# Late blocks of a token and channel MLP: the seventh second-layer product as seven of half size, and the last row's x by way of device memory

## The chip, the cores and the metric

The kernel runs on one core of one Trainium2 chip. The metric is device time in microseconds; lower is better. TensorE is called PE in the profile (PEld: its weight loads), VectorE DVE, ScalarE ACT, GpSimd POOL, SyncE SP.

## The reference

Eight batch rows. For each, eight heads of attention over 576 tokens with 64 elements each: the scores are scaled, those that lie more than tau under the row's largest are dropped, the rest goes through a softmax, and the weights multiply v. The heads side by side are x, 576 tokens by 512. Then an MLP over tokens, one over channels, both with a residual:

```
scores = scale * q @ k.T
scores = where(scores >= max(scores) - tau, scores, -1e9)
attn   = softmax(scores) @ v
x      = attn, heads side by side            # (8, 576, 512)
u      = x + (relu(x.T @ w_tok1) @ w_tok2).T # tokens: 576 -> 256 -> 576
out    = u + relu(u @ w_ch1) @ w_ch2         # channels: 512 -> 1536 -> 512
```

All of it is in 32-bit floats.

## The kernel before

**Main part.** Attention and the token MLP run row by row, 1 core, with tokens along the free dimension (`xT`, 128 x 4 x 576, holds x and then u of a row). A scheduler written into the kernel (`Scheduler`) holds every operation with a cost, a rank and its dependences, keeps a modelled clock per engine, and picks what can start first; the order in which it picks is the order of instructions on each engine. Nothing is reordered at run time: an engine that waits holds all that is queued behind it.

**The channel MLP is put off.** `NOW` says how many groups of 256 tokens of a row take it at once: two for row 0, one for rows 1 to 6, none for row 7. What is left of u is written to device memory by `spill(b)` (L533), except for row 7, whose u stays in `xTs[7]`.

**Late blocks.** After attention, when its memory is free, what was put off runs in five blocks of 512 tokens each (class `Late`, L1440): tokens of rows 1 and 2, rows 3 and 4, the last 64 tokens of all eight rows, rows 5 and 6, and row 7's first 512. `load` (L1448) fetches a block's u into one buffer `u`; the block of row 7 is marked `own` and reads `xTs[7]` in place. `turn_u` and `move_u` lay u out by tokens into `us` and `ut` for the residual.

**First layer** (`make_first`, L1530). For each of six slices j, the 2 x 2 product of halves is made with seven products and a number of sums (Strassen's scheme in Winograd's form) instead of eight products. Four sums of u (`sum_u`, buffer `t`) and three of the weights (`w1s`) feed it. Results, after relu, lie in `ga` (first half of the hidden layer) and `hidden_b` (second half).

**Second layer** (`make_second`, L1582). Again seven products. With a(i, k, m) the hidden activations (token half i, hidden half k, m one of two tiles of 128 tokens), the sums are S1 = a(1,0) + a(1,1), S2 = S1 - a(0,0), S3 = a(0,0) - a(1,0) and S4 = a(0,1) - S2. S1 and S2 have places of their own (`sum_place(0, m)` and `sum_place(1, m)`, in the memory of `x_sb` and `a`), S3 lies in a(1,0)'s place and S4 in a(0,1)'s. Six of the seven products are themselves made by `make_inner` (L1703) as seven products of half width and half depth, 3 matrix multiplies of 128 x 128 x 128 each (four of the six in the last block, where the products with a(0,0) and S1 are of full size). `make_inner` has the same scheme inside: its sums s1 to s4 are taken in place, on quarters of the left operand, one after another as the products that read them are done; its small results p1, u2, u3 lie in `small_place`, of which there are two sets, and its three weight sums in `inner_place(n)`, made once on DVE before the first second layer; the weights' quarter (0,1) is overwritten in place. The product x2 = a(0,1) times `side2(1, 0)` is the one that is of full size in all blocks: 6 matrix multiplies of 128 x 128 x 256 for each m. It stands first in the second layer, DVE adds it and the residual into o(0,0) (`y2`), and S4 is then taken in place:

```
x2[m] = plain(lambda m=m: a(0, 1, m), lambda: side2(1, 0), h2)
y2[m] = put_leave("dve", 0.42, lambda bank, m=m: add(four(o(0, 0, m)), four(bank), old(0, 0, m)), x2[m], ...)
s4[m] = sched.op("dve", 0.96, lambda m=m: sub(a(0, 1, m), a(0, 1, m), sum_place(1, m)), s2[m] + [x2[m]], 3)
```

Products fill eight PSUM banks; ACT or DVE takes each result out, and a bank is free for the next product when that is done.

Of the kernel before, what the change touches and what calls it, by code (L numbers as in the profile page):

```python
# [21 lines left out]
def kernel(  # L22
# [1127 lines left out]
    def make_row(b):  # L1150

        deps = [key_op("X", rank_of_group(b, p0, g)) for p0 in (0, 2) for g in range(3)]
        halves = make_tokens(b, token_mlp(b) if b else token_mlp(0, range(NP // 2, NP)), deps)
        if not b:
            for k in ("20", "21"):
                halves[k] = first_half[k] + halves[k]
        t = [x for x in sched.ops if x.eng == "pe" and x.row == b]
        tokens_x["1"] = [x for k, x in keyed.items() if k[0] == "tok" and k[1] == b and len(k) == 3]
        tokens_x["2"] = list(tokens_x["1"])
        outs = halves["20"] + halves["21"]  # L1160
        xreads[b] = xreads.get(b, []) + make_groups(b, halves) + outs
        if b < B - 1:
            xreads[b].append(put(("spill", b), sched.op("sp", 0.6, lambda: spill(b), outs, 2, dmas=(1, 383, 0.58))))
# [186 lines left out]

    flat = x_sb.rearrange("p t x -> p (t x)")
# [7 lines left out]
    def small_place(n, k):  # L1359
        if n == 0:  # L1360
            return small_a[:, k, :]
        return flat[:, 3 * TILE + P * k : 3 * TILE + P * k + P] if k < 2 else home("a")[:, TILE : TILE + P]

    def inner_place(n):
        at = [
            lambda: inner[0].rearrange("p k j x -> p (k j x)"),
            lambda: w1.rearrange("p t x -> p (t x)")[:, 0:QUARTER],
            lambda: w2.rearrange("p t x -> p (t x)"),
            lambda: home("xT")[:, 0:QUARTER],
            lambda: inner[1].rearrange("p k j x -> p (k j x)"),  # L1370
            lambda: inner_b.rearrange("p k j x -> p (k j x)"),
        ][n]()
        return at.rearrange("p (k j x) -> p k j x", k=3, j=HH)
# [7 lines left out]
    FACTORS = [lambda: w2s[:, 2], lambda: w2s[:, 1], lambda: side2(0, 1), lambda: side2(1, 1), lambda: side2(0, 0), lambda: w2s[:, 0]]  # L1381
# [9 lines left out]
    tokens = [x for x in pending if x.row == B - 1]  # L1391
# [12 lines left out]
    for n, y in enumerate(FACTORS):  # L1404
        quarter = lambda q, r, y=y: y()[:, HH * q : HH * q + HH, P * r : P * r + P]
        s = lambda k, n=n: inner_place(n)[:, k]
        steps = [
            lambda s=s, y=quarter: sub(s(0), y(0, 1), y(0, 0)),
            lambda s=s, y=quarter: sub(s(1), y(1, 1), s(0)),
            lambda s=s, y=quarter: sub(s(2), y(1, 0), s(1)),  # L1410
            lambda s=s, y=quarter: sub(y(0, 1), y(1, 1), y(0, 1)),
        ]
        done = []
        for step in steps:
            done.append(sched.op("dve", 0.55, step, free_all + done, 9))
        inner_weights.append(done)
# [21 lines left out]
    small_used = [[], []]  # L1438

    class Late:  # L1440


        def __init__(self, n):
            self.n = n
            self.own = groups[n][0][0] == B - 1
            self.us, self.ut, self.products = [None, None], [None, None], {}

        def load(self):  # L1448
            self.u = end.tile([P, NCC, 2 * GR], F32, tag="u", bufs=1, name=f"u_{self.n}")
            at = 0  # L1450
            for b, lo, n in groups[self.n]:
                src = spilled[b][:, :, lo - GR * NOW[b] :][:, :, 0:n] if b in spilled else xTs[b][:, :, lo : lo + n]
                nc.sync.dma_start(out=self.u[:, :, at : at + n], in_=src)
                at += n
# [11 lines left out]
        def block(self, k, n):  # L1466
            u = xTs[B - 1] if self.own else self.u
            return u[:, HC * k : HC * k + HC, GR * n : GR * n + GR]
# [13 lines left out]
        def turn_u(self, m, n):  # L1482
            pool = work if m == 0 else end
            if n == 0:
                self.us[m] = pool.tile([P, 2, 4, NCC * 32], F32, tag="us", bufs=1, name=f"us_{self.n}_{m}")
                self.ut[m] = pool.tile([P, 2, 4, NCC * 32], F32, tag="ut", bufs=1, name=f"ut_{self.n}_{m}")
            u = xTs[B - 1] if self.own else self.u
            nc.vector.transpose(
                out=self.us[m][:, n].rearrange("q a (c d) -> q c a d", c=NCC),
                in_=u[:, :, GR * n + P * m : GR * n + P * m + P].rearrange("q c (r a) -> q c a r", a=4),  # L1490
            )
# [5 lines left out]
        def make(self, before, spills):  # L1497
# [3 lines left out]
            if self.own:  # L1501
                ready = list(tokens)
            else:
                slots = [x for x in before if not x.own]
                free = slots[-1].reads if slots else []
                came = [spills[b] if b < B - 1 else x for b, _, _ in groups[n] for x in (tokens if b == B - 1 else [None])]
                count = len(groups[n])
                ready = [sched.op("sp", 1.2, self.load, came + free, -1, dmas=(count, 1024 // count, 0.6))]
# [16 lines left out]
            for j in range(HJ):  # L1525
                self.make_first(hidden, j, ready + sums, past.freed if past else {(i, k): free_all for i in range(2) for k in range(2)})
# [3 lines left out]
        def make_first(self, hidden, j, have, free):  # L1530
# [33 lines left out]
            z = put_bank(C, product(lambda: ws(0), lambda: us(0)), held((1, 1), (1, 0)) + [c6], rank)  # L1564
            x7 = put_more(y, C, product(lambda: w(1, 0), lambda: us(2), False), [c6] + have, 2)
            c7 = put_mid("act", 0.37, copy_to(u3), y, [x7] + used, 0)
            d5 = put_mid("dve", 0.42, lambda bank: add(gb(1), bank[:, 0:GR], u3), z, [z, c7] + free[1, 1])
            x4 = put_more(y, C, product(lambda: w(1, 1), lambda: us(3), False), [c7] + held((0, 1)), 2)
# [13 lines left out]
        def make_second(self, hidden, moved):  # L1582
# [59 lines left out]
            for m in range(2):  # L1642
                x2[m] = plain(lambda m=m: a(0, 1, m), lambda: side2(1, 0), h2)
                y2[m] = put_leave("dve", 0.42, lambda bank, m=m: add(four(o(0, 0, m)), four(bank), old(0, 0, m)), x2[m], [x2[m]] + moved[m])
                s4[m] = sched.op("dve", 0.96, lambda m=m: sub(a(0, 1, m), a(0, 1, m), sum_place(1, m)), s2[m] + [x2[m]], 3)
            ends = self.n == len(groups) - 1
            if ends:
                whole = []
                for n in (4, 5):
                    back = lambda q, r, n=n: FACTORS[n]()[:, HH * q : HH * q + HH, P * r : P * r + P]  # L1650
                    whole.append(sched.op("dve", 0.55, lambda back=back: sub(back(0, 1), back(1, 1), back(0, 1)), past_sums, 4))
                for m in range(2):
                    x1.append(plain(lambda m=m: a(0, 0, m), lambda: side2(0, 0), h11 + whole[:1]))
                    c1[m] = [put_leave("act", 0.37, lambda bank, m=m: nc.scalar.copy(out=p1_place(m), in_=bank[:, 0:HD]), x1[m], [x1[m]] + past_sums, 0)]
            else:
                c1 = self.make_inner(4, lambda m: a(0, 0, m), p1_place, [h11, h11], s2[0] + s2[1] + s3[0] + s3[1], [past_sums, past_sums])
                w5 = self.make_inner(5, lambda m: sum_place(0, m), lambda m: o(1, 1, m), s1, s2[0] + s2[1], [moved[0], moved[1]])
            w7_of = lambda m: w7[:, m, :]
            w4 = self.make_inner(0, lambda m: a(1, 1, m), lambda m: o(1, 0, m), [h2, h2], s1[0] + s1[1], [moved[0], moved[1]])
            w6 = self.make_inner(1, lambda m: sum_place(1, m), w6_place, s2, s4, [past_sums, past_sums])  # L1660
            w7s = self.make_inner(2, lambda m: a(1, 0, m), w7_of, s3, [], [past_sums, past_sums])
            w3 = self.make_inner(3, lambda m: a(0, 1, m), lambda m: o(0, 1, m), [[s4[0]], [s4[1]]], x2, [moved[0], moved[1]])
            all_second = []
            for m in range(2):
# [10 lines left out]
                if ends:  # L1675
                    b11 = joined(lambda eng, m=m: add(old(1, 1, m), old(1, 1, m), four(w7_of(m)), eng), [u3] + moved[m])
                    x5 = plain(lambda m=m: sum_place(0, m), lambda: w2s[:, 0], whole[1:] + s1[m] + small_used[0] + small_used[1][:1])
# [20 lines left out]
                (0, 1): x2 + s4 + self.products[3],  # L1698
# [4 lines left out]
        def make_inner(self, n, x, to, have, freed, writable):  # L1703
# [18 lines left out]
            p1, u2, u3 = [lambda k=k: small_place(n % 2, k) for k in range(3)]  # L1722
            used = small_used[n % 2]
# [31 lines left out]
            small_used[n % 2] = [d6, d7, d5, d4, d3]  # L1755
# [4 lines left out]
    spills = [key_op("spill", b) for b in range(B - 1)]  # L1760
# [36 lines left out]
```

## Time and profile before

| | us |
|---|---|
| median of 3 runs | 1220.56 |
| lowest, highest | 1220.19, 1221.44 |
| profiled execution, whole | 1218.91 |
| its span, first to last instruction | 1217.1 |
| PE busy in the span | 1191.5 |
| PE weight loads | 971.7 |
| DVE busy | 885.7 |
| ACT busy | 601.6 |
| POOL busy | 334.9 |

The span is that of one profiled execution; what lies around it, 1.8 us, is the difference to that execution's own time. Matrix multiplies are pipelined: each has a length in the trace, but the next one begins before it ends, so that the distance between two starts is what one costs. A row of the timeline puts equal instructions together and gives their count; one matrix multiply of the code is two instructions there. Of a group's row the numbers are: busy time, mean length of one in ns, idle time of the engine just before, and what ended it. The first late block begins at 862.73 us.

### The profile page before, as it was taken

What the parts mean: (1) busy time and instruction counts of PE and PEld (TensorE: products, weight loads), DVE (VectorE), ACT (ScalarE), POOL (GpSimd) and SP (SyncE); (2) the same over time, 40 slices, a digit from 0 to 9 for tenths busy, and PEclk for the clock granted to TensorE, in tenths of its full rate; (3) what the DMA queues carried; (4) which work ended last, traced back from release to release, by engine and by line L of the source; (5) the groups of instructions that cost most, each with busy time, mean ns of one, the idle gap of its engine ahead of it and who ended that gap; (6) DMA issues with size and microseconds to landing.
All of it is one profiled execution on the core that took longest, in us unless ns stands there. A gap on an engine that the chain in (4) does not pass through costs nothing.

```text
span 1217.1 us, 21941 instructions
## 1 busy us (share of the span) xinstructions
PE 1191.5 (98%) x7913; PEld 971.7 (80%) x7913; DVE 885.7 (73%) x1497; ACT 601.6 (49%) x1360; POOL 334.9 (28%) x524
## 2 busy tenths in 40 slices
PE   8888999999999999999999999999999999999998
PEld 8656788777777777777777777778899898999988
DVE  7788996677778677767866876742677586776856
ACT  6988864564656565465556566431232323223130
POOL 3676543333333424433333333410100000000000
PEclk9999999999999999999999999999999999999999
DMA  8656867768777776776876875850210302120010
GB/s 147 138 124 171 230 170 164 159 138 189 162 171 152 184 159 156 191 165 138 196 166 131 189 177 118 198 139 22 53 36 1 91 15 70 35 54 17 31 40 36
DMA packets 325372, 149.78 MB, mean 123 GB/s; under 512 B 223824, under 2 KB 318032, under 8 KB 325264
## 3 DMA queue, kind: packets, MB, share of 16 engines
q1 hardware_dynamic: 323104, 147.64, 53.0%
q8 instruction: 63, 1.03, 0.3%
q10 hardware_dynamic: 2160, 0.74, 0.2%
q14 instruction: 45, 0.37, 0.1%
HBM read 47.32 MB, written 13.50 MB: 50 GB/s over the span
## 4 chain that ended last, share of the span: by engine, by line
PE 85%; DVE 6%; ACT 2%; SPq 2%; DMA 2%; issue 1%; POOL 1%; ACTq 0%; DVEq 0%; POOLq 0%
PE bank L1436 29%; PE bank L1060 12%; PE sc L850 11%; PE bank L984 11%; PE bank L371 9%; PE bank L478 5%; PE bank L460 5%; PE bank L366 3%; DVE mx L867 2%; SPq L328 1%; DVE T L316 1%; PE warm L677 1%; ACT e L883 1%; DMA eT<-T 1%; POOL e L286 1%
## 5 line engine op out<-in xcount | busy, mean ns | idle before, releaser
L286 POOL TENSOR_SCALAR e<-e,rr 128x576 f32<-128x576 f32 x288 | 219.0, 780 | 210.5 <-DVE rr L278 197.4
L883 ACT ACTIVATE e<-sc,bias 128x576 f32<-128x576 f32 x288 | 194.7, 743 | 161.9 <-POOL bias L873 160.8
L893 ACT ACTIVATE e<-e,ntau 128x576 f32<-128x576 f32 x288 | 220.7, 780 | 0.2
L867 DVE TENSOR_REDUCE mx<-sc 128x2 f32<-128x1152 f32 x144 | 187.9, 1345 | 40.7 <-PE sc L850 40.4
L316 DVE STREAM_TRANSPOSE T<-e 128x1152 f32<-128x1152 f32 x126 | 170.4, 1362 | 38.5 <-DMA eT<-T 17.3
L1060 PE MATMUL bank<-xT,wc 128*128 128x256 f32 x768 | 178.1, 383 | 2.7 <-ACT g L1065 1.6
L1060 PEld LDWEIGHTS bank<-xT,wc 128*128 128x128 f32 x768 | 142.7, 190 | 31.2 <-issue 4.4
L850 PE MATMUL sc<-kT,qT 64*128 64x192 f32 (+1 forms) x1920 | 165.0, 332 | 1.4 <-ACT e L883 1.0
L850 PEld LDWEIGHTS sc<-kT,qT 64*128 64x128 f32 (+1 forms) x1920 | 138.0, 176 | 30.9 <-issue 19.1
L371 PE MATMUL bank<-eT,lv 128*64 128x384 f32 (+1 forms) x1024 | 135.1, 406 | 0.0
L371 PEld LDWEIGHTS bank<-eT,lv 128*64 128x64 f32 x1024 | 73.6, 137 | 50.6 <-issue 45.6
L873 POOL TENSOR_SCALAR bias<-mx,toff 128x2 f32<-128x2 f32 x144 | 41.3, 287 | 168.7 <-DVE mx L867 165.0
L984 PE MATMUL bank<-wc,g 128*128 128x256 f32 x336 | 77.9, 382 | 0.0
L478 PE MATMUL bank<-w,a 128*128 128x192 f32 (+1 forms) x256 | 72.9, 418 | 3.1 <-DVE g L1068 1.3
L984 PEld LDWEIGHTS bank<-wc,g 128*128 128x128 f32 x336 | 62.9, 190 | 13.2 <-issue 2.5
L460 PE MATMUL bank<-x_sb,w 128*128 128x256 f32 x320 | 72.5, 381 | 1.0 <-DVE x_sb L445 0.7
L1557 ACT COPY temps<-bank 128x256 f32<-128x256 f32 x90 | 33.4, 371 | 78.2 <-PE bank L1436 78.1
L460 PEld LDWEIGHTS bank<-x_sb,w 128*128 128x128 f32 x320 | 60.2, 190 | 10.6 <-DVE x_sb L445 1.0
L478 PEld LDWEIGHTS bank<-w,a 128*128 128x128 f32 x256 | 43.4, 189 | 22.7 <-issue 3.9
L1065 ACT ACTIVATE g<-bank 128x256 f32<-128x256 f32 x56 | 21.6, 385 | 80.4 <-PE bank L1060 79.4
L893 ACT ACTIVATION_READ_ACCUMULATOR e<-e,ntau 128x1 f32 x288 | 58.8, 204 | 0.0
L984 PE MATMUL bank<-w2s,g 128*128 128x256 f32 x252 | 58.2, 381 | 0.0
(180 smaller groups left out, 1811.2 us busy)
## 6 DMA issues: line engine op xcount, KB each, us to landing
eT<-T SPq DMA_DIRECT2D x504, 144.0 KB, 3.0
w2s<-in_moe_w_ch_dram SPq DMA_DIRECT2D x24, 512.0 KB, 4.1
lk<-in_k_dram SPq DMA_DIRECT2D x122, 72.0 KB, 2.8
ut<-us SPq DMA_DIRECT2D x136, 64.0 KB, 2.1
lq<-in_q_dram SPq DMA_DIRECT2D x120, 72.0 KB, 3.0
lv<-in_v_dram SPq DMA_DIRECT2D x112, 72.0 KB, 2.5
out_dram<-us SPq DMA_DIRECT2D x30, 256.0 KB, 2.3
spill<-xT SPq DMA_DIRECT2D x6, 640.0 KB, 4.1
```

The source lines that it names most:

```text
L286: nc.gpsimd.tensor_scalar(out=eh, in0=eh, scalar1=rr[:, h : h + 1], scalar2=1.0, op0=ALU.mult, op1=ALU.mult)
L316: nc.vector.transpose(out=T.rearrange("p a (c x) -> p c a x", c=NK), in_=e.rearrange("p (c a x) -> p c a x", c=NK, a=4))
L371: nc.tensor.matmul(to[r], lhsT=lv[:, j, :], rhs=e[j], start=False, stop=(c == NI - 1), skip_group_check=True)
L460: nc.tensor.matmul(to, lhsT=w1[:, t, P * m : P * m + P], rhs=x(t), start=(t == 0), stop=(t == NT - 1), skip_group_check=len(products) > 1,)
L478: nc.tensor.matmul(bank[:, n * i : n * i + n], lhsT=hidden[b][:, m, P * c : P * c + P], rhs=w2[:, m, lo : lo + n], start=(m == 0), stop=(m ...
L850: nc.tensor.matmul(sc[h][rows, f, HT * k : HT * k + HT], lhsT=qT[r, cols], rhs=kT[r, HT * f : HT * f + HT], start=True, stop=True, skip_gr ...
L867: nc.vector.tensor_reduce(out=mx[:, h], in_=sc[h][:, :, 0 : 2 * HT].rearrange("p f (k x) -> p k f x", k=2), axis=AX.XY, op=ALU.max)
L883: nc.scalar.activation(out=eh, in_=part[h], func=AF.Prelu, bias=bias[:, h], scale=SCALE, alpha=STEEP)
L893: nc.scalar.activation(out=eh, in_=eh, func=AF.Exp, bias=ntau, accum_out=rs[:, h, 0:1])
L984: nc.tensor.matmul(bank[:, 0:HD], lhsT=x[:, j, :], rhs=y[:, j, :], start=j == 0, stop=j == HJ - 1)
L1060: nc.tensor.matmul(bank[:, 0:n], lhsT=wc1[:, j, c, :], rhs=uT[:, c, GR * i : GR * i + n], start=(c == 0), stop=(c == NCC - 1))
L1436: nc.tensor.matmul(to, lhsT=l, rhs=r, start=start and x == 0, stop=x == len(pairs) - 1, skip_group_check=not start)
```

## The change

In the four blocks before the last, the product a(0,1) times `side2(1, 0)` is made by `make_inner` too, as number 6: per block, 12 matrix multiplies of 256 columns become 21 of 128, with sums on DVE and copies on ACT as the other six have. The last block keeps it at full size, and there the overwritten quarter of `side2(1, 0)` is restored first, as for the two others (`whole`).

Because the new product needs a(0,1) unchanged by S4 while it is made, S4 now goes into S1's place, after all products of S1 (number 5) are done; in the last block it stays in a(0,1)'s place (`of3` in the diff is the place that holds S4).

The weight sums of the new product need memory. Row 7's u is written to device memory as the others' is (`spill` for all rows), the blocks with row 7 load it from there, `own` goes, and the second buffer of `xT` becomes `late_y`, which holds these weight sums and three more sets of small places (five in all; products 0 to 6 use sets 0, 1, 0, 1, 2, 3, 4).

Beside that, in the first layer each product waits for the one sum of u that it reads instead of for all four, and the second product of a slice comes after the first.

```diff
-        if b < B - 1:
-            xreads[b].append(put(("spill", b), sched.op("sp", 0.6, lambda: spill(b), outs, 2, dmas=(1, 383, 0.58))))
+        xreads[b].append(put(("spill", b), sched.op("sp", 0.6, lambda: spill(b), outs, 2, dmas=(1, 383, 0.58))))
...
+    def home_of_last():
+        if "y" not in homes:
+            homes["y"] = work.tile([P, NP, S], F32, tag="xT", name="late_y").rearrange("p c x -> p (c x)")
+        return homes["y"]
...
+        if n > 1:
+            return home_of_last()[:, QUARTER + P * (3 * n - 6 + k) : QUARTER + P * (3 * n - 6 + k) + P]
...
+            lambda: home_of_last()[:, 0:QUARTER],
...
-    FACTORS = [lambda: w2s[:, 2], ..., lambda: w2s[:, 0]]
+    FACTORS = [lambda: w2s[:, 2], ..., lambda: w2s[:, 0], lambda: side2(1, 0)]
...
-            done.append(sched.op("dve", 0.55, step, free_all + done, 9))
+            done.append(sched.op("dve", 0.55, step, free_all + done + ([key_op("spill", B - 1)] if n == 6 else []), 9))
...
-    small_used = [[], []]
+    SMALL = [0, 1, 0, 1, 2, 3, 4]
+    small_used = [[] for _ in range(5)]
...
-                src = spilled[b][:, :, lo - GR * NOW[b] :][:, :, 0:n] if b in spilled else xTs[b][:, :, lo : lo + n]
+                src = spilled[b][:, :, lo - GR * NOW[b] :][:, :, 0:n]
...
-            x2 = put_bank(C, product(lambda: w(0, 1), lambda: u(1, 0)), held((0, 0)), rank)
+            x2 = put_bank(C, product(lambda: w(0, 1), lambda: u(1, 0)), held((0, 0)) + [y], rank)
...
-            x6 = put_more(y, C, product(lambda: ws(1), lambda: us(1), False), [c1] + have, 2)
+            x6 = put_more(y, C, product(lambda: ws(1), lambda: us(1), False), [c1, sums[1]] + have, 2)
...
-            for m in range(2):
-                x2[m] = plain(lambda m=m: a(0, 1, m), lambda: side2(1, 0), h2)
-                y2[m] = put_leave("dve", 0.42, ...)
-                s4[m] = sched.op("dve", 0.96, lambda m=m: sub(a(0, 1, m), a(0, 1, m), sum_place(1, m)), s2[m] + [x2[m]], 3)
...
             if ends:
...
-                for n in (4, 5):
+                for n in (6, 4, 5):
...
+                for m in range(2):
+                    x2[m] = plain(lambda m=m: a(0, 1, m), lambda: side2(1, 0), h2 + whole[:1])
+                    y2[m] = put_leave("dve", 0.42, ...)
+                    s4[m] = sched.op("dve", 0.96, lambda m=m: sub(a(0, 1, m), a(0, 1, m), sum_place(1, m)), s2[m] + [x2[m]], 3)
...
             else:
-                c1 = self.make_inner(4, lambda m: a(0, 0, m), p1_place, ...)
                 w5 = self.make_inner(5, lambda m: sum_place(0, m), lambda m: o(1, 1, m), s1, ...)
+                for m in range(2):
+                    s4[m] = sched.op("dve", 0.96, lambda m=m: sub(sum_place(0, m), a(0, 1, m), sum_place(1, m)), s2[m] + h2 + self.products[5], 2)
+                c1 = self.make_inner(4, lambda m: a(0, 0, m), p1_place, ...)
+                w2 = self.make_inner(6, lambda m: a(0, 1, m), lambda m: o(0, 0, m), [h2, h2], s4, [moved[0], moved[1]])
+                for m in range(2):
+                    y2[m] = joined(lambda eng, m=m: add(four(o(0, 0, m)), four(o(0, 0, m)), old(0, 0, m), eng), w2[m] + moved[m])
...
-            w3 = self.make_inner(3, lambda m: a(0, 1, m), ..., x2, [moved[0], moved[1]])
+            w3 = self.make_inner(3, of3, ..., read3, [moved[0], moved[1]])
...
-    spills = [key_op("spill", b) for b in range(B - 1)]
+    spills = [key_op("spill", b) for b in range(B)]
```

More of the change, by code (lines that the diff above doesn't have):

```diff
@@ L1390 @@
     last = [x for x in pending if x.row < B - 1]
-    tokens = [x for x in pending if x.row == B - 1]
     free_all = pending + state["stores"] + state["adds"]
@@ L1466, in block @@
         def block(self, k, n):
-            u = xTs[B - 1] if self.own else self.u
-            return u[:, HC * k : HC * k + HC, GR * n : GR * n + GR]
+            return self.u[:, HC * k : HC * k + HC, GR * n : GR * n + GR]
         def sum_u(self, n):
@@ L1500, in make @@
             past = before[-1] if before else None
[L1501 to L1508, printed above, removed]
+            free = before[-1].reads if before else []
+            came = [spills[b] for b, _, _ in groups[n]]
+            count = len(groups[n])
+            ready = [sched.op("sp", 1.2, self.load, came + free, -1, dmas=(count, 1024 // count, 0.6))]
             self.reads = []
@@ L1525, in make, with make_first @@
             for j in range(HJ):
-                self.make_first(hidden, j, ready + sums, past.freed if past else {(i, k): free_all for i in range(2) for k in range(2)})
+                self.make_first(hidden, j, ready, sums, past.freed if past else {(i, k): free_all for i in range(2) for k in range(2)})
             self.reads += sums + self.first
             self.make_second(hidden, moved)
-        def make_first(self, hidden, j, have, free):
+        def make_first(self, hidden, j, have, sums, free):
             rank = 3 + 2 * self.n
@@ L1641, in make_second @@
             x1 = []
-            for m in range(2):
-                x2[m] = plain(lambda m=m: a(0, 1, m), lambda: side2(1, 0), h2)
-                y2[m] = put_leave("dve", 0.42, lambda bank, m=m: add(four(o(0, 0, m)), four(bank), old(0, 0, m)), x2[m], [x2[m]] + moved[m])
-                s4[m] = sched.op("dve", 0.96, lambda m=m: sub(a(0, 1, m), a(0, 1, m), sum_place(1, m)), s2[m] + [x2[m]], 3)
             ends = self.n == len(groups) - 1
+            w7_of = lambda m: w7[:, m, :]
+            rests = [past_sums, past_sums]
             if ends:
                 whole = []
-                for n in (4, 5):
+                for n in (6, 4, 5):
                     back = lambda q, r, n=n: FACTORS[n]()[:, HH * q : HH * q + HH, P * r : P * r + P]
@@ L1652, in make_second @@
                 for m in range(2):
-                    x1.append(plain(lambda m=m: a(0, 0, m), lambda: side2(0, 0), h11 + whole[:1]))
+                    x2[m] = plain(lambda m=m: a(0, 1, m), lambda: side2(1, 0), h2 + whole[:1])
+                    y2[m] = put_leave("dve", 0.42, lambda bank, m=m: add(four(o(0, 0, m)), four(bank), old(0, 0, m)), x2[m], [x2[m]] + moved[m])
+                    s4[m] = sched.op("dve", 0.96, lambda m=m: sub(a(0, 1, m), a(0, 1, m), sum_place(1, m)), s2[m] + [x2[m]], 3)
@@ L1697, in make_second @@
                 (1, 1): flat_of(s1) + self.products[0],
-                (0, 1): x2 + s4 + self.products[3],
+                (0, 1): s4 + (self.products[6] if 6 in self.products else x2 + self.products[3]),
             }
@@ L1721, in make_inner @@
             weights = inner_weights[n]
-            p1, u2, u3 = [lambda k=k: small_place(n % 2, k) for k in range(3)]
-            used = small_used[n % 2]
+            p1, u2, u3 = [lambda k=k: small_place(SMALL[n], k) for k in range(3)]
+            used = small_used[SMALL[n]]
             def product(l, r, start=True):
```

28 lines of the change are left out of this document (14 added, 14 removed).

## The prediction

> **What bounds the kernel now.** I read the page first: its totals, the slices, the engines' shares of the chain that ended last.
>
> ```profile
> span 1217.1 us, 21941 instructions
> PE 1191.5 (98%) x7913; PEld 971.7 (80%) x7913; DVE 885.7 (73%) x1497; ACT 601.6 (49%) x1360; POOL 334.9 (28%) x524
> ...
> PE   8888999999999999999999999999999999999998
> ...
> PE 85%; DVE 6%; ACT 2%; SPq 2%; DMA 2%; issue 1%; POOL 1%; ACTq 0%; DVEq 0%; POOLq 0%
> ```
>
> TensorE (PE) carries 85% of the chain. The built order of the changed kernel equals that of before on every engine up to the first late block, so only the late stage matters. There, busy time by stretch (columns: stretch, its length, then busy time and instructions of PE, PEld, DVE, ACT, POOL, the clock, DMA share, GB/s); the last row is one whole middle block.
>
> ```profile
> 802.70:862.70 60.00, 60.00 (x284) 49.70 (x283) 19.71 (x28) 7.99 (x19) 4.51 (x5) 1.00 0.20 59
> 904.20:1038.50 134.30, 134.30 (x866) 124.62 (x865) 96.17 (x224) 38.48 (x107) 0.00 (x0) 1.00 0.15 40
> 1108.00:1190.00 82.00, 81.89 (x525) 75.88 (x524) 59.53 (x135) 22.33 (x62) 0.00 (x0) 1.00 0.10 27
> 1038.50:1108.10 69.60, 69.60 (x446) 64.57 (x445) 50.21 (x117) 19.68 (x55) 0.00 (x0) 1.00 0.19 46
> ```
>
> PE is never empty there, at full clock. DVE is busy 50.21 of 69.60 us and ACT 19.68. So the end moves by what PE has to do, plus what it must wait for. The timeline of PE gives the prices (start, length, then what; each matrix multiply of the code stands as two instructions):
>
> ```profile
> 862.73 1.89 PE L1436 MATMUL bank<-u,wc 128*128 128x256 f32 x8
> ...
> 1108.08 5.34 PE L1436 MATMUL bank<-wc,hidden_b 128*128 128x256 f32 x24
> 1113.26 1.03 PE L1436 MATMUL bank<-xT,wc 128*128 128x256 f32 x4
> 1114.12 0.83 PE L1436 MATMUL bank<-inner,ga 128*128 128x128 f32 x6
> 1114.79 0.83 PE L1436 MATMUL bank<-wc,ga 128*128 128x128 f32 x6
> ...
> 1210.04 2.75 PE L1436 MATMUL bank<-w2s,x_sb 128*128 128x256 f32 x12
> ```
>
> Lengths overlap; starts count. The product that is replaced (24 instructions, both halves m) holds PE from 1108.08 to 1113.26, 5.18 us, 0.216 per instruction. One half-size product (6 instructions of 128 columns) goes from 1114.12 to 1114.79, 0.67. A first-layer product of 4 instructions takes 0.86.
>
> **The sum on PE.** Each of the four blocks before the last gives up 5.18 us and gets seven times 0.67 = 4.69, so 0.49 less, four times: 1.96 us. The last block keeps the full-size form. No PE work is added elsewhere.
>
> How much idle time is there besides? A late block's first layer has 6 x 7 products at 0.86: 181 us for five blocks. Full-size products are 5 x 5.18 plus 2 x 5.18 in the last block, 36.3. Half-size ones: 4 x 42 + 28 = 196 at 0.67, 131.3. Together 348.6 us. The stage runs from 862.73 to 1210.04 + 2.59 = 1212.63: 349.9 us. So about 1.3 us is idle or rounding, and that is all that a better order could give on top.
>
> **What the seven add on DVE and ACT.** Per block: four sums over quarters, four small sums out of banks, one small sum, three copies on ACT. The sum of the old y2 stays (from SBUF instead of from a bank), and so does S4.
>
> ```profile
> L951 DVE TENSOR_TENSOR ga<-ga 128x384 f32<-128x384 f32 x10 | 5.4, 553 | 0.2
> L948 DVE TENSOR_TENSOR us<-us,ut 128x256 f32<-128x256 f32 x6 | 2.5, 422 | 0.2
> L948 DVE TENSOR_TENSOR small_a<-bank,small_a 128x128 f32<-128x128 f32 x6 | 1.7, 290 | 0.7 <-PE bank L1436 0.6
> L951 DVE TENSOR_TENSOR hidden_b<-hidden_b,x_sb 128x768 f32<-128x768 f32 x1 | 0.9, 950 | 0.0
> L948 DVE TENSOR_TENSOR late_x<-late_x,small_a 128x128 f32<-128x128 f32 x1 | 0.3, 281 | 0.0
> L1738 ACT COPY small_a<-bank 128x128 f32<-128x128 f32 x14 | 3.7, 266 | 6.7 <-PE bank L1436 6.6
> ```
>
> DVE: 4 x 0.553 + 4 x 0.290 + 0.281 = 3.65 us, so 53.9 of some 69.1 us. ACT: 3 x 0.266 = 0.8 us. Both lie beside PE work on average. The question is where DVE must answer in time, and the built order shows two tight places in each of the four blocks.
>
> First place: S4 now stands where S1 stood, so it may start only when all seven products of S1 are done, and the sums inside the new product come after it. In the built order 17 DVE operations lie between the sixth product of S1 and the fifth of the new one: ten small (2.9), four of 256 columns (1.7), the two S4 (1.9), the first quarter sum (0.55). Back to back that is 7.05 us. PE does in that time 5 half-size and 6 first-layer products, 5 x 0.67 + 6 x 0.86 = 8.5 us, of which the first 0.94 is gone before DVE can use the sixth product:
>
> ```profile
> 1049.68 0.83 PE L1436 MATMUL bank<-inner,ga 128*128 128x128 f32 x6
> ...
> 1050.62 0.62 DVE L948 TENSOR_TENSOR small_a<-bank,small_a 128x128 f32<-128x128 f32 x2 [0.33 <-PE bank L1436]
> ```
>
> So 7.05 us of DVE in 7.57: half a microsecond to spare, and I cost this at nothing. The cover is thin, though.
>
> Do operations on DVE take their whole length, one after the other?
>
> ```profile
> 1042.07 1.02 DVE L951 TENSOR_TENSOR ga<-ga 128x384 f32<-128x384 f32 x2
> 1074.40 0.56 DVE L948 TENSOR_TENSOR hidden_b<-hidden_b 128x384 f32<-128x384 f32 x1 [0.73 <-PE bank L1436]
> 1074.99 0.56 DVE L951 TENSOR_TENSOR hidden_b<-hidden_b 128x384 f32<-128x384 f32 x1
> 1075.81 0.62 DVE L948 TENSOR_TENSOR small_a<-bank,small_a 128x128 f32<-128x128 f32 x2 [0.26 <-PE bank L1436]
> 1076.46 0.29 DVE L948 TENSOR_TENSOR w<-bank,small_a 128x128 f32<-128x128 f32 x1
> ```
>
> Two that do not depend on each other begin 0.47 us apart (1.02 - 0.55), a dependent one 0.59 after the first. So 7.05 is about right or a little long.
>
> Second place: the sixth product inside the new one is followed after two others by its third, which waits for three small DVE sums. The same pattern exists today:
>
> ```profile
> 1074.87 0.83 PE L1436 MATMUL bank<-w,ga 128*128 128x128 f32 x6
> ...
> 1076.88 0.86 PE L1436 MATMUL bank<-wc,ga 128*128 128x128 f32 x6
> ```
>
> The sixth starts at 1074.87, its sums at 1075.81, the last sum ends at 1076.75, and the third product starts at 1076.88 instead of 1074.87 + 3 x 0.67 = 1076.88, its 0.86 showing 0.03 lost. Four more such places: 0.12 us. Where DVE is still at something else, it costs more:
>
> ```profile
> 1145.37 0.83 PE L1436 MATMUL bank<-wc,hidden_b 128*128 128x128 f32 x6
> 1146.31 0.94 PE L1436 MATMUL bank<-late_x,hidden_b 128*128 128x128 f32 x6
> ...
> 1146.30 0.74 PEld L1436 LDWEIGHTS bank<-late_x,hidden_b 128*128 128x128 f32 x6 [0.29 <-DVE small_a L948]
> ```
>
> Here PE lost 0.27 us (0.94 between starts against 0.67) behind a small sum. That was in the block whose second layer changes order, so it may go or come again; with its own length, 0.94 against 0.83, it lost 0.37. I take between 0 and 0.37 for each of the four blocks and 0.05 as the value, nearest to the 0.03 row: 0.2 us, ends 0 and 1.5.
>
> **What moves besides.** The last row's x goes out to device memory and comes back:
>
> ```profile
> 863.64 0.55 DVE L489 TENSOR_TENSOR xT<-xT,bank 128x384 f32<-128x384 f32 x1
> 867.60 10.27 SPq L1495 DMA_DIRECT2D ut<-us  x16
> 899.18 1.22 SPq L1453 DMA_DIRECT2D u<-spill  x2
> ...
> u<-spill SPq DMA_DIRECT2D x6, 512.0 KB, 4.6
> ```
>
> The spill can be issued at 864.2, behind the sum at 863.64. On SP it precedes the 16 moves, whose results are not read for 30 us. Its 1.18 MB should land within 4.6 x 1180/512 = 10.6 us, by 875. Who waits: on DVE the four quarter differences of the new product's weights, which overwrite that x; in the built order they stand near the end of block 0's first layer, after 890. Behind them on DVE are the last sums of that layer. Cost nothing; were the landing 10 us later still, PE would stop. The last block no longer reads x in place but loads it (two issues, 4.6 us), as blocks 1 and 3 do now behind the previous first layer, some 5 us ahead of its first sums: nothing. The four weight differences (2.2 us of DVE in block 0) and one restoring difference in the last block lie beside PE. The five sets of small places remove waits that the rows do not show as PE's idle time: nothing.
>
> At the start of each second layer PE had 5.18 us that needed no sum; now four half-size products, 2.68 us.
>
> ```profile
> 1038.47 5.34 PE L1436 MATMUL bank<-wc,hidden_b 128*128 128x256 f32 x24
> ...
> 1039.79 1.03 DVE L948 TENSOR_TENSOR x_sb<-ga,hidden_b 128x384 f32<-128x384 f32 x2 [0.70 <-ACT ga L1556]
> ```
>
> The first product that needs one of the last sums of S1 is three more on, 4.7 us in, and today these sums are done at 1040.82, 2.4 us into the layer. Nothing.
>
> Sum: -1.96 + 0.2 = -1.8 us (ends -2.0 and -0.5, or -3 with all idle gone). Against the profiled execution, span 1217.1, it is 1215.3; that execution took 1218.91 in all, 1.65 under the median of the runs, so I apply the difference to the median: 1220.56 - 1.8 = **1218.8**. That is 0.15%, inside the 0.2% (2.4 us) that a measurement of this kernel can tell from no change.
>
> **Rivals.** (a) The order improves as well: the idle 1.3 us, the two rows at 1146 among it, goes to below half. Then -1.96 - 0.7 or more, 1217.9 or lower: faster by over 0.2%. For it: the sums' waits are now given one by one, so that PE has more to choose from. Against: new tight places. Chance 0.16.
>
> (b) DVE sets the pace at the first tight place. If its 17 operations take 0.1 us more each (as dependent ones do beside independent ones, 0.59 against 0.47), 1.7 us, PE waits 1.2 us in each of four blocks: -1.96 + 4.8, 1223.4, slower. It decides from 1.1 us per block on. Against it: the half microsecond to spare, counted with full lengths. Chance 0.08.
>
> (c) Stalls of 0.3 to 0.5 us per block, as at 1146, eat the gain: 1220 to 1220.6, no change. Chance 0.10.
>
> (d) Halving the width does not halve the time, because each narrow product has as many weight loads. Were a half-size product paced by loads that do not overlap, the 0.74 us of the loads' row above instead of 0.67, seven would cost 5.18, the full-size price, and the change would gain nothing on PE and lose its stalls: 1220.8. The 0.67 between starts stands all through the stage, loads included, so 0.01. The Trainium skill, TensorE: Matmul & The Clock Gate, section Back-to-back issue gap, speaks for this rival: it gives measured 81 ns per product at 128 columns and 131 ns at 512, far from proportional. An estimate from it, by a straight line between, is 98 ns at 256 columns, so that seven half-size products would cost 1.45 times the full-size one. The trace does not agree: 0.112 us against 0.216 per instruction here.
>
> **The numbers.** The forecast itself has 0.65. Faster 0.16 (a); same 0.65 + 0.10 + 0.01 = 0.76; slower 0.08 (b). The range runs from the low side of (a), 1217.8, to the far end of (c), 1220.6; it leaves out (b) and some of (a).
>
> **What would show it.** In the changed trace: the two rows of 24 instructions on hidden_b gone from four blocks and in each a group `late_y,hidden_b`; middle blocks about 69.1 us instead of 69.6; PE busy throughout, last product ending near 1210.8. DVE some 54 us per block. I am wrong if PE shows idle time before the products on `late_y,hidden_b` or behind the S4 sums, if DVE waits for the spill before writing `late_y`, or if the middle blocks differ by other than half a microsecond.

## The result, and the profile after

The changed kernel takes 1216.96 us (median of 15 runs; before, 15 runs beside them, 1219.84): 0.9977 of before, 95% interval [0.9966, 0.9988]. Timed again later it was 0.9984 [0.9972, 0.9996]. So it is faster, by about 2 to 3 us, more than the 1.8 us of the forecast, whose range (from 1217.8) it leaves on the low side. The forecast counted from 1220.56, the median of three runs; the 15 runs of the kernel before lie 0.72 us lower. Against them the gain is 2.88 us.

The page of the profiled execution (1216.17 us in all) against the lines of before:

```profile
span 1214.4 us, 22144 instructions
PE 1189.0 (98%) x7985; PEld 971.5 (80%) x7985; DVE 901.6 (74%) x1538; ACT 603.4 (50%) x1372; POOL 333.8 (27%) x524
...
PE   8888999999999999999999999999999999999998
...
PE 84%; DVE 2%; ACT 1%; DMA 0%; SPq 0%; issue 0%; DVEq 0%; POOL 0%
```

PE has 72 more instructions (four times 42 in place of 24) and is 2.5 us less busy. DVE has 16 us more. The row by stretch (same columns as before) of the block that corresponds to the forecast's middle block:

```profile
1037.40:1106.50 69.10, 69.10 (x464) 64.62 (x463) 53.17 (x125) 20.20 (x57) 0.00 (x0) 1.00 0.19 47
```

69.10 us instead of 69.60, as forecast, and DVE 53.2 (forecast 53.9). The timeline of PE in the changed kernel (start, length, what): the start of the late stage, some of the half-size products that stand for the row of 24 instructions, and the last product:

```profile
862.80 1.89 PE L1442 MATMUL bank<-u,wc 128*128 128x256 f32 x8
...
1060.64 1.03 PE L1442 MATMUL bank<-t,w1s 128*128 128x256 f32 x4
1061.50 0.83 PE L1442 MATMUL bank<-late_y,hidden_b 128*128 128x128 f32 x6
...
1065.04 0.83 PE L1442 MATMUL bank<-late_y,hidden_b 128*128 128x128 f32 x6
...
1067.05 0.83 PE L1442 MATMUL bank<-wc,hidden_b 128*128 128x128 f32 x6
...
1207.59 2.76 PE L1442 MATMUL bank<-w2s,x_sb 128*128 128x256 f32 x12
```

From 862.80 to 1207.59 + 2.59 = 1210.18 the late stage takes 347.38 us; before it was 349.90. That is 2.52 less, where the forecast had 1.96 of work less and 0.2 of stalls more.

**Where the stalls went.** The distance between two starts, less 0.216 us for each instruction of 256 columns and 0.112 for each of 128, is what PE lost there. Before, four places lost more than 0.05 us: 0.09 (at 938.16), 0.20 (1029.73 and the row behind it), 0.37 (1146.31) and 0.25 (1206.01), 0.91 in all. After, two: 0.10 (937.27) and 0.25 (1203.56), 0.35. So 0.56 us of stalls are gone, and 1.96 + 0.56 = 2.52. What PE's weight loads waited for in the late stage (engine, what, us, times, longest), first before, then after:

```profile
PEld bank L1436 <- ACT temps L1557: 0.3, 1, 0.3
PEld bank L1436 <- DVE small_a L948: 0.3, 1, 0.3
PEld bank L1436 <- DVE hidden_b L951: 0.2, 1, 0.2
```

```profile
PEld bank L1442 <- DVE hidden_b L951: 0.2, 1, 0.2
```

The stalls at 1029.73 (a product behind ACT's copy of the one before) and at 1146.31 (behind a small sum) do not come back in any block. The rest, 0.25 us, is behind the last product: 1217.1 - 1212.63 = 4.47 us before, 1214.4 - 1210.18 = 4.22 after. 2.52 + 0.25 = 2.77 us less is 0.9977 of 1219.84.

**How the experiments are read.** Single times differ by several us from run to run. Two windows (0 to 100 and 100 to 200 us; the column behind the busy times is the granted clock) show where they part, first in the changed kernel, then in an experiment that ran 1221.72 us:

```profile
0.00:100.00 100.00, 87.41 (x716) 66.21 (x717) 81.19 (x141) 85.07 (x179) 56.35 (x97) 1.00 0.71 142
100.00:200.00 100.00, 95.05 (x696) 74.03 (x694) 87.02 (x131) 70.20 (x151) 54.00 (x68) 1.00 0.74 187
```

```profile
0.00:100.00 100.00, 88.54 (x713) 67.70 (x713) 80.20 (x140) 83.52 (x176) 55.59 (x95) 0.98 0.67 139
100.00:200.00 100.00, 95.20 (x673) 72.70 (x672) 87.52 (x130) 70.54 (x152) 53.58 (x67) 0.98 0.74 186
```

At 0.98 in the first 200 us, long before the change acts, its late stage began at 866.24 instead of 862.80. Over all 14 profiles that start goes with the granted clock of the whole execution: 862.57 to 863.28 at 1.0, 864.01 to 865.04 at 0.999, 865.73 at 0.997, 866.24 at 0.996. The length of the late stage itself repeats: the changed kernel's was 347.38 in both of its profiles. So the experiments are compared by that length, from the start of the first first-layer product to the end of the last product. A time without a median is that of one run; `[y]` is the edit that puts the second product of a first-layer slice, x2, behind the first, y.

| kernel | late stage, us | time, us |
|---|---|---|
| before | 349.90 | 1219.84 (median of 15) |
| changed | 347.38 | 1216.96 (median of 15) |
| before, first-layer part | 349.26 | 1219.51 |
| before, `[y]` alone | 349.24 | 1221.72 |
| before, last row by memory | 349.53 | 1219.91 |
| changed, x2 full size again | 349.21 | 1217.78 |
| changed, first layer as before | 349.79 | 1220.28 |
| changed, two sets of small places | 368.52 | 1239.36 |
| changed, S4 written twice | 351.21 | 1220.49 |
| changed, last block's a(0,1) too | 346.97, 346.98 | 1218.51; later 1219.10 (median of 12) |
| changed, and a(0,0) too | 349.40 | 1220.62 |
| changed, last block's a(0,0) only | 347.69 | 1217.52 (median of 11) |

### The profile page after: what moved, and what is told of

Same layout as the page of the kernel before. It is cut to its first block, busy times and chain, and to the rows that moved or that the text cites. A ratio compares the mean times of both kernels' runs of the same rounds, so it can differ in the third digit from the quotient of the medians.

```text
span 1214.4 us, 22144 instructions
## 1 busy us (share of the span) xinstructions
PE 1189.0 (98%) x7985; PEld 971.5 (80%) x7985; DVE 901.6 (74%) x1538; ACT 603.4 (50%) x1372; POOL 333.8 (27%) x524
## 4 chain that ended last, share of the span: by engine, by line
PE 84%; DVE 2%; ACT 1%; DMA 0%; SPq 0%; issue 0%; DVEq 0%; POOL 0%
PE bank L1442 29%; PE bank L1060 12%; PE bank L984 11%; PE sc L850 10%; PE bank L371 9%; PE bank L478 5%; PE bank L460 5%; PE bank L366 3%; PE bank L1075 2%; DVE mx L867 1%; ACT e L883 0%; PE bank L441 0%; SPq L328 0%; DVE T L316 0%; DMA lk<-in_k_dram 0%; DMA eT<-T 0%
## 5 line engine op out<-in xcount | busy, mean ns | idle before, releaser
L460 PEld LDWEIGHTS bank<-x_sb,w 128*128 128x128 f32 x320 | 60.2, 190 | 10.6 <-DVE x_sb L445 1.0
L1442 PE MATMUL bank<-u,wc 128*128 128x256 f32 x240 | 60.5, 379 | 0.0
L1442 PE MATMUL bank<-t,wc 128*128 128x256 f32 x240 | 60.5, 379 | 0.0
```

The costliest lines, as they stand in the source:

```text
L460: nc.tensor.matmul(to, lhsT=w1[:, t, P * m : P * m + P], rhs=x(t), start=(t == 0), stop=(t == NT - 1), skip_group_check=len(products) > 1,)
L1442: nc.tensor.matmul(to, lhsT=l, rhs=r, start=start and x == 0, stop=x == len(pairs) - 1, skip_group_check=not start)
```

## The experiments

The theory at the start (A): 1.96 us of work, and the stall ahead of the last block goes because that block loads its x. The rivals: the first layer's finer list of waits (B), or the second layer's own parts (C).

**1. First-layer part alone**, on the kernel before:

```
- x2 = put_bank(C, ..., held((0, 0)), rank)
+ x2 = put_bank(C, ..., held((0, 0)) + [y], rank)
- x6 = put_more(y, C, ..., [c1] + have, 2)            # have: x and all sums
+ x6 = put_more(y, C, ..., [c1, sums[1]] + have, 2)   # z, x7, x4 likewise
```

> The kernel before with only the first layer's dependences of the change (each product waits for the one sum of u that it reads; the second product of a slice comes after the first). The late stage on PE, from the first start of block 0 to the end of the last product, took 349.9 us before and 347.4 after. Theory A (the change takes 1.96 us of PE work away; the other half microsecond is a stall of 0.37 us in the block ahead of the last, which goes because the last block loads its x like the others): no part of that is here, 349.8 to 349.9. Rival B (the finer dependences of the first layer took the stalls away): 349.4.

349.26, 0.64 less than before. No operation of the second layer was touched, and the stalls of 0.09, 0.20 and 0.37 us are all gone.

**2. The changed kernel with this part undone**:

> The changed kernel with the first layer's dependences of before. Theory A: 347.4 us for the late stage, as after, to 347.5. Rival B: the half microsecond comes back, 347.9.

349.79: 2.41 us more than the changed kernel, and only 0.11 less than before. No theory had that. The three old stalls do not return with the old list; a new one stands in each of the four blocks. PE and DVE in one block of it:

```profile
999.00 0.83 PE L1442 MATMUL bank<-late_y,hidden_b 128*128 128x128 f32 x6
1000.22 0.94 PE L1442 MATMUL bank<-w,late_a 128*128 128x128 f32 x6 [0.39 <-DVE late_y L948]
1000.99 0.83 PE L1442 MATMUL bank<-wc,hidden_b 128*128 128x128 f32 x6
```

```profile
999.12 0.56 DVE L951 TENSOR_TENSOR x_sb<-x_sb,late_a 128x384 f32<-128x384 f32 x1
999.87 0.62 DVE L948 TENSOR_TENSOR late_y<-bank,late_y 128x128 f32<-128x128 f32 x2 [0.19 <-PE bank L1442]
```

1000.22 - 999.00 is 1.22 instead of 0.67, and the next row comes 0.10 late: 0.65 us in each of the four blocks, 2.6. The product right behind the sixth product inside the new seven waits for the small sum that reads that sixth product. It is the forecast's second tight place, but one product stands there between the sixth and the third where the forecast counted two, and it is the one that waits. In the changed kernel (1065.04 to 1067.05 above) two stand there, and nothing is lost. What the waiting product lacks is a PSUM bank: in the built program it writes the same bank as the sixth product, and the event that it waits for is the end of the sum that reads this bank out.

**3. The last row by way of memory, alone**:

```
- if b < B - 1:                      # spill
+ if True:
...
- self.own = groups[n][0][0] == B - 1
+ self.own = False
...                                  # load: from device memory for all rows
```

> The kernel before with only row 7's x written to device memory and loaded again by the blocks that need it (two sets of small places, the full-size product). Theory A: the 0.37 us stall ahead of the last block goes, 349.4 to 349.5 us for the late stage. Rivals B and C (C: the seven half-size products and the five sets of small places take the stalls away): 349.9.

349.53, as theory A has it: exactly the 0.37 us at 1146.31 go; the others stay.

**4. Everything but the seven** (x2 of full size in all blocks, S4 in its old place):

> The changed kernel with the seventh product at full size in all blocks again and S4 in the place of a(0,1); row 7 by way of device memory, four sets of small places and the finer dependences stay. Theory A: PE work as before, stall gone, 349.4 us. Rival C: 349.9. Both: middle blocks 69.6 us against 69.1 after.

349.21. The first-layer part and the way by memory together give 0.69, hardly more than the first-layer part's 0.64: both take away the same 0.37. From here to the changed kernel, 1.83 us, is the seven with S4's new place and the fifth set, against 1.96 of work by the rates.

**5. `[y]` alone.** The list has two edits in it: x2 ordered behind y, and the sums given one by one. The built order of the changed kernel with its sums as one list again is the same as the changed kernel's on every engine, so there the second edit does nothing. (On the kernel before it does move some products, from 1107 us on, but experiment 1 with it and this one without it differ by 0.02 us in the stage.) One line on the kernel before:

```
- x2 = put_bank(C, ..., held((0, 0)), rank)
+ x2 = put_bank(C, ..., held((0, 0)) + [y], rank)
```

> The kernel before with one thing of the change alone: the first layer's x2 is ordered behind y (the list of what x2 waits for gets y added); the sums stay one list. Stage of before 349.90, with visible stalls of 0.09, 0.20, 0.37 and 0.25 us; with the whole first-layer part alone it was 349.26. Theory A (this one line reorders TensorE's products so that the stalls ahead of the last block go): 349.2 to 349.4. Rival B (the split sums are needed for it): 349.8 to 350.0.

349.24, -0.66: theory A. All three stalls are gone; PE's weight loads wait once:

```profile
PEld bank L1436 <- DVE hidden_b L951: 0.2, 1, 0.2
```

What the line does is seen in PE's timeline at the same place of the third block, before and with the line:

```profile
1026.18 1.89 PE L1436 MATMUL bank<-u,w1s 128*128 128x256 f32 x8
1027.91 1.89 PE L1436 MATMUL bank<-u,wc 128*128 128x256 f32 x8
1029.73 1.99 PE L1436 MATMUL bank<-t,w1s 128*128 128x256 f32 x8
```

```profile
1029.63 1.03 PE L1436 MATMUL bank<-u,w1s 128*128 128x256 f32 x4
1030.49 1.03 PE L1436 MATMUL bank<-u,wc 128*128 128x256 f32 x4
1031.36 1.03 PE L1436 MATMUL bank<-t,w1s 128*128 128x256 f32 x4
```

Before, two slices of the first layer go abreast, equal products in pairs (x8), so that a product comes right behind the copy that it needs (the wait for `temps` above); with the line they are staggered. The stall at 1146.31 goes with the new order too; which of the moved products it owes that to was not looked into.

**6. Two sets of small places** in the changed kernel:

```
- SMALL = [0, 1, 0, 1, 2, 3, 4]
+ SMALL = [0, 1, 0, 1, 0, 1, 0]
```

> The changed kernel with two sets of small places, used in turn by all seven half-size sevens, instead of five. Theory A (the waits that the sets remove are no idle time of TensorE, the forecast's cost of nothing): stage 347.4 to 347.6 against 347.38. Rival B (they are: a product that reuses a set waits for the last sum of the one two before, as the 0.65 us in each block of the kernel whose first layer was put back): 0.3 to 0.65 us in each of four blocks, 348.6 to 350.

368.52, 21.1 us more: 5.3 in each block. Rival B had the sign, with a tenth of the size. The whole block, and one of its stalls on PE and DVE:

```profile
976.80:1051.30 74.50, 71.19 (x463) 65.13 (x463) 53.07 (x126) 20.23 (x57) 0.00 (x0) 1.00 0.17 43
```

```profile
1019.37 0.83 PE L1442 MATMUL bank<-w,ga 128*128 128x128 f32 x6
1021.30 0.94 PE L1442 MATMUL bank<-wc,ga 128*128 128x128 f32 x6 [1.10 <-DVE w L948]
```

```profile
1020.31 0.62 DVE L948 TENSOR_TENSOR small_a<-bank,small_a 128x128 f32<-128x128 f32 x2 [0.72 <-PE bank L1442]
1020.96 0.29 DVE L948 TENSOR_TENSOR w<-bank,small_a 128x128 f32<-128x128 f32 x1
```

DVE has the same 53 us of work as in the changed kernel, in 74.5 instead of 69.1 us. PE waits for a small sum, DVE idles 0.72 us for the product: the two take turns, since by the code no other seven may start before a set is free. In this block the sevens go two at a time, and the one that is left over, of a(1,0), runs alone: it has the longest stall, the one shown.

**7. S4 written twice** in the four blocks, with the order kept:

```
- sub(sum_place(0, m), a(0, 1, m), sum_place(1, m))
+ [sub(sum_place(0, m), a(0, 1, m), sum_place(1, m)) for _ in range(2)]
```

> The changed kernel, but in the four blocks ahead of the last each S4 sum (0.95 us on VectorE) is written twice in a row, four such operations instead of two; the order of everything else stays. The late stage, from its first first-layer product to the end of the last matrix product, took 347.38 us in the changed kernel. Two added operations take 1.74 us (0.86 between starts of independent ones: 1057.85, 1058.71). In the changed kernel the quarter sum behind S4 starts 0.30 us late because VectorE waits for TensorE, and ends at 1060.73 for a product that starts at 1061.50: some 0.3 + 0.7 = 1.0 us spare. Theory A (VectorE is the near bound at this first tight place, with 1.0 us to spare): 0.75 us lost per block, stage 350.3, with an idle row before the product on late_y,hidden_b. Rival B (half a microsecond to spare, as forecast): 1.2 lost per block, 352.3. Rival C (VectorE is nowhere near the bound, other work fills in): 347.4 to 348.

351.21, +3.83: 0.96 per block, between theory A's 0.75 and rival B's 1.2. PE and DVE at the place:

```profile
1063.00 1.03 PE L1442 MATMUL bank<-t,w1s 128*128 128x256 f32 x4
1064.74 0.94 PE L1442 MATMUL bank<-late_y,hidden_b 128*128 128x128 f32 x6 [0.71 <-DVE hidden_b L948]
```

```profile
1060.22 1.94 DVE L951 TENSOR_TENSOR x_sb<-hidden_b,x_sb 128x768 f32<-128x768 f32 x2
1062.08 1.94 DVE L951 TENSOR_TENSOR x_sb<-hidden_b,late_a 128x768 f32<-128x768 f32 x2
1063.94 0.28 DVE L948 TENSOR_TENSOR us<-bank,small_a 128x128 f32<-128x128 f32 x1
1064.14 0.55 DVE L948 TENSOR_TENSOR hidden_b<-hidden_b 128x384 f32<-128x384 f32 x1
```

The added time is 1.74 us by the changed kernel's 0.86, or 1063.94 - 1060.22 = 3.72 for four, less 1.72 for two, 2.0 by these rows; 0.96 came through, so 0.8 to 1.0 was spare. The first tight place is real, and it holds with more room than the half microsecond of the forecast.

**8. The last block too.** Three kernels on top of the change: its a(0,1) product as seven, with S4 in the loaded x's place; that and the a(0,0) product; the a(0,0) product only.

```
- x2[m] = plain(lambda m=m: a(0, 1, m), lambda: side2(1, 0), ...)          # last block
+ w2 = self.make_inner(6, lambda m: a(0, 1, m), lambda m: o(0, 0, m), ...)
- x1.append(plain(lambda m=m: a(0, 0, m), lambda: side2(0, 0), ...))       # second and third kernel
+ c1 = self.make_inner(4, lambda m: a(0, 0, m), p1_place, ...)
```

> The changed kernel with the last block treated as the other four: its product of a(0,1) too as seven of half size, S4 in the place of the loaded x, and one restoring difference fewer. By the rates the work of the late stage falls by 5.18 - 7 x 0.67 = 0.49 us, from 347.38 to 346.9. Theory A (work on TensorE decides): 346.8 to 347.0. Rival B (in the last block no next first layer fills the gaps, so the chains of sums show): stalls of 0.25 to 0.94 us take it back, 347.1 to 347.9.

> As the kernel before it in this call, with the last block's product of a(0,0) as seven of half size as well, so that only one full-size pair is left in it. Theory A (work decides): another 0.49 us less, 346.4. Rival B (last block short of other work): no gain over the kernel before it, 346.9 to 348, with idle rows on TensorE after 1180.

> The changed kernel with the last block's product of a(0,0), not of a(0,1), as seven of half size; the other stays full size, so S4 stays where it was and the built order of the last matrix products is that of the changed kernel. Theory A (work decides as long as the tail stays): stage 347.38 - 0.49 = 346.9, end of the span 4.2 us behind it, ratio to before 0.9973. Rival B (chains of sums in the last block): stalls of 0.3 us or more in it, stage 347.2 to 348, ratio 0.9977 or above.

The first had 346.97, 0.41 of the 0.49. The second had 349.40 and the third 347.69: there the small sums show. No next first layer lies behind the last block to fill the gaps; that this is the reason is argued and not tested. Weight loads of the second, then of the third:

```profile
PEld bank L1442 <- DVE us L948: 1.8, 3, 0.6
PEld bank L1442 <- DVE late_x L948: 0.6, 2, 0.3
```

```profile
PEld bank L1442 <- DVE w L948: 0.5, 1, 0.5
PEld bank L1442 <- DVE late_a L948: 0.4, 1, 0.4
```

The first was timed beside the changed kernel and the third:

> The changed kernel again, timed beside the next two: 0.9977 of before as measured, some 2.8 us less; stage 347.4.

> The kernel with the last block's a(0,1) product as seven of half size too: its stage took 346.97 us, 0.41 less than the changed kernel's, but VectorE still ran 1.2 us behind the last matrix product instead of 0.95, and the time from the last product to the end of the span was 4.4 instead of 4.2. Theory A: 0.2 us less than the changed kernel, ratio to before 0.9974 to 0.9977, not told apart from the changed kernel. Rival B (the longer tail takes all of it): the same ratio or up to 0.9980.

The changed kernel 0.9984 [0.9972, 0.9996], the first 0.9999 [0.9988, 1.001], the third 0.9984 [0.9974, 0.9994]. The 0.41 us on PE did not come out as time. In its second profile 4.49 us lie behind the last product (1217.2 - 1212.71) instead of 4.2, as DVE has more sums left; that takes 0.3 of it. The rest of the median is not explained by the late stage. The granted clock of its 12 runs was 0.9975 in the median, that of the changed kernel's 12 runs 1.0; the late stage of the profiled run began at 865.73. And some of its runs had up to 3.1 us outside the span, where the changed kernel's have 1.8. Why is open. No version was found that beats the changed kernel.

## Why the prediction was wrong

**Where the miss comes from.** The forecast was 1218.8, the median 1216.96: 1.84 us lower. Of that, 0.72 is the start, 1220.56 from three runs where 15 gave 1219.84; 0.76 are the stalls, 0.56 fewer instead of 0.2 more; 0.25 is the end of the program, which the forecast left unchanged; the remaining 0.11 is within the spread of the runs. Counted from 1219.84 the range would have reached down to 1217.08, and the median would still lie just below it.

**The work on PE: right.** 1.96 us by four times (5.18 - 7 x 0.67); the middle blocks are 69.10 us, and without the seven but with all the rest the stage is 1.83 longer, the seven having brought 0.10 us of stall of its own at 937.27. An estimate from the figures of the Trainium skill (TensorE: Matmul & The Clock Gate, Back-to-back issue gap) had the seven dearer than the full-size product; the trace does not agree, it has 0.67 between the new rows too (1061.50 and its neighbours).

**The stalls: this is the step that failed.** "I take between 0 and 0.37 for each of the four blocks and 0.05 as the value", 0.2 us in all, with ends 0 and 1.5, were stalls added, and the value of the old ones was left as it was. The runs show 0.56 us fewer. The idle 1.3 us was about right as a ceiling: 0.91 in the four places, the rest mostly rounding of the rates. Rival (a), at 0.16, had the direction. Its size, -2.66 or more with over half of the 1.3 us gone, came out as -2.52 in the stage; only with the 0.25 us at the end is it passed, and that was luck. The reason given for (a), the sums' waits one by one, is wrong: undone in the changed kernel, they change no engine's order. What the forecast gave no word to was `[y]`: 0.66 us alone, and 2.41 us in the changed kernel. The built order showed that the first layer's pairs became staggered; that each pair stood right behind ACT's copy was to be read from the rows at 1029.73, and the stall at 1146.31 was weighed only as something that "may go or come again". None of the signs of being wrong that the forecast named appeared: they were new stalls, a wait for the spill, and middle blocks off by other than half a microsecond. None looked for an old stall that goes.

**The second tight place: right place, wrong value.** With the first layer as before it costs 0.65 us in each block, more than the end of 0.37; with `[y]` nothing. Without this line rival (c), stalls that eat the gain, would have come true in its outcome: the stage is 0.11 us shorter than before, though the stalls are longer than its 0.3 to 0.5.

**The first tight place and rival (b): right.** Half a microsecond to spare was said, 0.8 to 1.0 was there (experiment 7). By that the 17 operations would have to take some 0.05 us more each before the place cost anything, an estimate.

**The sets of small places.** "Nothing" was the forecast's price, since it looked for their worth in waits of before, and there it found none. Their worth lies in the seventh product that they carry: 21 us in experiment 6.

**The last row by memory: nothing lost, as said.** The spill was issued and landed long before its place is written (`late_y` first at 894.1):

```profile
864.85 0.38 SPq L537 DMA_DIRECT2D spill<-xT  x1
...
spill<-xT SPq DMA_DIRECT2D x1, 1152.0 KB, 4.4
```

4.4 us instead of the estimated 10.6. The estimate scaled the 4.6 us of a 512 KB load by size, but those loads go out in pairs (899.18, two issues in 1.22 us), with 1024 KB under way together. (It also set 1180 beside 512, two different units; 1152 by 512 gives 10.4.) By itself the way by memory saves 0.37 us in the stage, which the first layer's line saves as well, and it gives the 0.25 us at the end.

**The end: 0.25 us not foreseen.** 4.47 to 4.22 us behind the last product. The three kernels that read the last row in place have 4.42 to 4.47, the changed kernel and the six others that load it and end with the same products 4.16 to 4.25. The traces show where it lies. The last sum and the last store stand equally far behind the last product in both. Then SyncE waits for the transfers' eight completion semaphores one after another, and the transfers take these in turn. Before, there are 1165 transfers: the last store has the fifth semaphore, its wait is met at 1216.07, and three more waits follow at 1216.13, 1216.20 and 1216.26. The way by memory adds three transfers, one spill and two loads. With 1168 the last store has the eighth, its wait is met at 1213.57, and no other follows. The three waits are 0.19 of the 0.25 us.

## What to carry to other kernels

Where an engine is full and the order is laid down ahead, a part of a change that computes nothing, one more entry in a list of waits, can be worth as much as the work that is saved: here 0.66 us alone, and 2.4 us with the new products, against 1.96 us of work saved. So value the reordering where it lands: list every place where the busy engine loses time, and ask of each who precedes it in the new order. And a part that removes no wait of today may be what keeps the new part from waiting; ask what it would cost without it.

## What the runs showed of the hardware

A clock of 0.98 in the first 200 us went with a start of the late stage that was some 3 us later, while the stage, at 1.00 in the profiles of both kernels, repeated to 0.01 us (347.38 twice, 346.97 and 346.98): for a change that acts in one stage, its length says what 15 whole runs can hardly tell.

An SP transfer of 1152 KB to device memory landed in 4.4 us; a load of 512 KB, issued beside a second one, in 4.6 us (before). The 512 KB loads go out in pairs, so these rows give no time by size.

At the end of the program each wait of SyncE for a semaphore that is already there took 0.06 us (1216.07 to 1216.26, three waits), so even the number of transfers ahead of the last one can shift the time.
